# Start of a fused attention and MoE kernel: the first tile's queries loaded alone, the other head split on GpSimd, filler transposes

## The chip, the core and the metric

The kernel runs on one core of one Trainium2 chip. The metric is the device time of one execution in microseconds (us). Five engines work side by side, each through its own queue in order: TensorE (PE, with its weight loads as PEld), VectorE (DVE), ScalarE (ACT), GpSimd (POOL) and SyncE (SP), which here only issues DMAs.

## What is computed

Attention with pooled queries, then two MoE-like layers. Shapes: batch 2, 8 heads, 1152 keys, head size 64, 576 pooled queries per head.

```python
def _attn_ref(q, k, v):
    B, H, S, D = q.shape                       # 2, 8, 1152, 64
    q_pool = q.reshape(B, H, S // 2, 2, D).mean(axis=3)
    scores = (1 / np.sqrt(D)) * np.matmul(q_pool, k.transpose(0, 1, 3, 2))
    scores = scores - np.max(scores, axis=-1, keepdims=True)
    attn = np.exp(scores)
    attn = attn / (np.sum(attn, axis=-1, keepdims=True) + 1e-09)
    return np.matmul(attn, v)

x = attn_out.transpose(0, 2, 1, 3).reshape(B * S2, H * D)
h = x @ w_in;  x = np.maximum(0.01 * h, h) @ w_out        # 512 -> 2048 -> 512
p = probs / probs.sum(-1)
out = sum(p[:, e] * (np.maximum(x @ w1[e], 0) @ w2[e]) for e in range(4))
```

All operands are float32. The kernel splits each into a high part (rounded to the fp32r type) and a low part (the rest) and multiplies the parts.

## The kernel before

The attention works on 8 pairs of heads (batch x 4 pairs), each pair in 9 tiles of 128 query rows by 1152 keys: tiles 0 to 3 belong to head 0, tile 4 to both heads, tiles 5 to 8 to head 1. A running number i counts tiles over all pairs, so tile 9 is the first of pair 1. Per tile, with the names used below:

- **S(i)**, line 346: 6 matmuls (12 for tile 4 of pair 0) of queries and keys into three PSUM banks, which all tiles share; then the **eviction** on DVE (line 349), which scales into `e` and takes the row's extreme.
- **exp(i)** on ACT (line 355), a small sum on DVE (line 359), a reciprocal on DVE (line 363) and **norm(i)** on POOL (line 365).
- **T(i)**, line 386: 9 transposes on PE; ACT copies them out as the high part (line 390), DVE subtracts for the low part (line 98 through `lo`).
- The product with v (line 413), spread over later tiles; `done` (lines 421 to 424) writes `xh` and `xl`, on POOL for nearly all tiles.

The order on each engine is the order in which the program emits its instructions (`manual_schedule`). The main loop emits for step i: S(i+2) and its eviction (i+3 from i = 6 on, line 511), sum(i+1), T(i) with norm(i+1) behind its first three transposes, some products with v, exp(i+2), and then what `steps[i]` holds. `steps` are the pieces of preparing a later pair: `prep_pair(n)` gives a list of pieces, and `begin_at` says at which step the list starts (pair 0's v at step 0, pair 1 at step `P1` = 1, pair 2 at step 8). For pairs 1 and up the preparation is: pool the queries (`q_add`, POOL), high part of the keys (`k_hi`, ACT), low part (`k_lo`, POOL, one instruction of 128x1152, followed by four DMAs on SP that spread both parts over the partitions), `q_hi` (ACT), `q_lo` (DVE for pair 1, followed by four DMAs on SP), then v (`v_hi` ACT, `v_lo`). S(9) needs pair 1's key DMAs and the two DMAs of its queries of head 0; all stand in SP's one queue, keys first.

Pair 0 has a start of its own, `first_pair`: its queries and keys are loaded twice, to partitions 0 to 63 and to 64 to 127, by eight DMAs of 288 KB on SP in the order queries of head 0, keys of head 0, queries of head 1, keys of head 1, with v behind them. Then q_add, q_lo and k_lo of both heads run on DVE and q_hi and k_hi on ACT, all before the main loop, and v_lo of pair 0 runs on DVE. While the data comes, PE runs 28 filler transposes of the identity (line 449).

Of the kernel before, what the change touches and what calls it, by code (L numbers as in the profile page):

```python
# [11 lines left out]
F32 = mybir.dt.float32  # L12
# [15 lines left out]
CW = 384  # L28
# [5 lines left out]
def f32(ap):  # L34
    return ap.bitcast(F32)
# [3 lines left out]
def tile_kernel(ctx: ExitStack, tc: tile.TileContext, q, k, v, w_in, w_out, probs, w1, w2, out):  # L39
    nc = tc.nc  # L40
    PE, ACT, DVE, POOL, SP = nc.tensor, nc.scalar, nc.vector, nc.gpsimd, nc.sync

    def at(name, off, shape, dt=F32R):

        return nc.alloc_sbuf_tensor_at(name, [128, *shape], dt, offset=BASE + 4 * off).ap()
# [9 lines left out]
    qst = [at(f"qst{i}", 18432 + 2560 * i, [2, 2, SQ + 64]) for i in range(2)]  # L55
# [33 lines left out]
    def hi(eng, dst, src):  # L89
        if eng is ACT:  # L90
            ACT.copy(dst, src)  # L91
        elif eng is POOL:
            POOL.tensor_scalar(dst, src, 1.0, 1.0, op0=ALU.mult, op1=ALU.mult)
        else:
            DVE.tensor_copy(dst, src)

    def lo(eng, dst, src, high):
        eng.tensor_tensor(dst, src, f32(high), op=ALU.subtract)  # L98
# [53 lines left out]
    def load_a():  # L152
        f = next(a_next, None)
        if f is not None:
            SP.dma_start(wa_raw[f % 2], w_in[f].bitcast(I32))
# [37 lines left out]
    with ExitStack() as actx:  # L193
# [3 lines left out]
        def transposed():  # L197
            return PS[:, next(bank_t), :CW].rearrange("p (a b) -> p a b", a=3)
# [12 lines left out]
        def two_heads(n, name):  # L211
            return [kv[name, h, n % 2] for h in range(2)]

        def load_qk(n):
            if n >= len(pairs):
                load_a()
                load_a()
                return
            b, p = pairs[n]
            rk, rq = rk_b, rq_b.rearrange("p (a b) -> p a b", a=2)  # L220
            SP.dma_start(rk, k[b, p])
            SP.dma_start(rq, q[b, p])
            raw[n] = (rk, rq)

        def load_v(n):
            if n >= len(pairs):
                return
            b, p = pairs[n]
            raw_v[n] = rv_b.rearrange("p (a h d) -> p a h d", a=NKB, h=2)
            SP.dma_start(raw_v[n], v[b, p])  # L230

        def first_pair():

            b, p = pairs[0]
            ks = kst[0] = two_heads(0, "k")
            rk = [rk_b, e_b[4]]
            rq = [t.rearrange("p (a b) -> p a b", a=2) for t in (rq_b, e_b[3])]
            up, down = slice(0, 64), slice(64, 128)
            for h in range(2):
                src = slice(h * 64, h * 64 + 64)  # L240
                for d in (up, down):
                    SP.dma_start(rq[h][d], q[b, p, src])
                for d in (up, down):
                    SP.dma_start(rk[h][d], k[b, p, src])
            load_v(0)

            def q_add(h):
                DVE.tensor_tensor(rq[h][:, 0], rq[h][:, 0], rq[h][:, 1], op=ALU.add)

            def q_hi(h):  # L250
                hi(ACT, qst[0][:, 0, h, h * 64:h * 64 + SQ], rq[h][:, 0])

            def q_lo(h):
                cs = slice(h * 64, h * 64 + SQ)
                lo(DVE, qst[0][:, 1, h, cs], rq[h][:, 0], qst[0][:, 0, h, cs])

            def k_hi(h, c):
                cs = slice(c * CW, (c + 1) * CW)
                hi(ACT, ks[h][:, cs], rk[h][:, cs])

            def k_lo(h, c):
                cs = slice(c * CW, (c + 1) * CW)
                lo(DVE, ks[h][down, cs], rk[h][down, cs], ks[h][down, cs])
            return q_add, q_hi, q_lo, k_hi, k_lo

        def prep_pair(n):


            e_q, e_v = DVE if n == 1 else POOL, DVE if n == 0 else POOL
            rk, rq = raw.get(n, (None, None))  # L270

            def k_hi():
                kh = k_hi_of[n] = kh_b[n % 2]
                hi(ACT, kh, rk)

            def k_lo():
                kh = k_hi_of[n]
                ks = kst[n] = two_heads(n, "k")
                lo(POOL, rk.bitcast(F32R), rk, kh)
                for h in range(2):  # L280
                    r = slice(h * 64, h * 64 + 64)
                    SP.dma_start(f32(ks[h][0:64]), f32(kh[r]))
                    SP.dma_start(f32(ks[h][64:128]), rk[r])

            def q_add():
                POOL.tensor_tensor(rq[:, 0], rq[:, 0], rq[:, 1], op=ALU.add)

            def q_hi():
                hi(ACT, rq[:, 1].bitcast(F32R), rq[:, 0])

            def q_lo():
                lo(e_q, rq[:, 0].bitcast(F32R), rq[:, 0], rq[:, 1])
                t = qst[n % 2]
                for h in range(2):
                    r = slice(h * 64, h * 64 + 64)
                    hi(POOL, qmid[n % 2][r, r], rq[r, 0, (SQ - 64) * (1 - h):][:, :64])
                    for d in (slice(0, 64), slice(64, 128)):
                        SP.dma_start(f32(t[d, :, h, h * 64:h * 64 + SQ]), rq[r])

            def v_hi(h):  # L300
                if h == 0:
                    vst[n] = [t.rearrange("p (a b) -> p a b", a=NKB) for t in two_heads(n, "v")]
                a = h * 64
                hi(ACT, vst[n][h][:, :, a:a + 64], raw_v[n][:, :, h, :])

            def v_lo(h):
                a, c = h * 64, 64 - h * 64
                lo(e_v, vst[n][h][:, :, c:c + 64], raw_v[n][:, :, h, :], vst[n][h][:, :, a:a + 64])

            if n == 0:  # L310
                return [[lambda: v_hi(0)], [lambda: v_lo(0)], [lambda: v_hi(1)], [lambda: v_lo(1), lambda: load_v(1)]]
            return [[q_add, k_hi], [k_lo], [q_hi], [q_lo, lambda: load_qk(n + 1)], [lambda: v_hi(0)],
                    [lambda: v_lo(0), lambda: v_hi(1)], [lambda: v_lo(1), lambda: load_v(n + 1)]]

# [2 lines left out]

        AVD, AVB = 1.07, {1: 0.5}

        P0, P1, P2 = 10, 1, 8  # L320

        L2 = 6

# [115 lines left out]
                av.pop(0)[1]()  # L439

        with tc.manual_schedule():

            DVE.memset(warm, 0.0)
            ACT.activation(warm, warm, AF.Exp)
            q_add, q_hi, q_lo, k_hi, k_lo = first_pair()

            wps = transposed()
            for _ in range(28):
                PE.transpose(wps[:, 0], ident, ident)
            q_add(0)  # L450
            q_hi(0)
            q_lo(0)
            for c in range(3):
                k_hi(0, c)
                k_lo(0, c)
            q_add(1)
            q_hi(1)
            at = dict.fromkeys(("s", "exp", "sum", "norm"), 0)

            def upto(what, emit, i):  # L460
                first = {"exp": "s", "sum": "exp", "norm": "sum"}
                while at[what] <= i and at[what] < (at[first[what]] if what in first else len(tiles)):
                    emit(at[what])
                    at[what] += 1

            upto("s", emit_s, 0)
            upto("exp", emit_exp, 0)
            q_lo(1)
            for c in range(3):
                k_hi(1, c)  # L470
            upto("s", emit_s, 1)
            upto("sum", emit_sum, 0)
            upto("norm", emit_norm, 0)
            for c in range(3):
                k_lo(1, c)
            upto("exp", emit_exp, 1)
            load_qk(1)

# [24 lines left out]


            begin_at = {9 * m - P0: m for m in range(3, len(pairs))} | {0: 0, P1: 1, P2: 2}
            steps = {}
            for i, (n, t) in enumerate(tiles):
                if i in begin_at:
                    for d, fs in enumerate(prep_pair(begin_at[i])):
# [274 lines left out]
    with tc.manual_schedule():  # L784
# [24 lines left out]
        for what, *args in order:  # L809
            what(*args)  # L810
            if what is product:
                p, name = args
# [4 lines left out]
                elif name == "P2" and p or name == "P7" and p == NPAIR - 1:  # L817


                    n = p - (name == "P2")  # L820
# [31 lines left out]
```

## Time and profile before

| what | us |
|---|---|
| median of 3 runs | 868.78 (866.94 to 868.99) |
| the profiled execution | 866.99 |
| its span, first to last instruction | 865.2 |
| PE busy | 829.0 (96%) |
| DVE / ACT / POOL busy | 587.4 / 435.6 / 403.6 |

The span is cut into slices by some views, with the busy share of each engine, the clock granted to TensorE (1.00 is 2.4 GHz, 0.50 is 1.2 GHz) and what the DMAs moved. A timeline row gives start, duration, engine, line, operation, output <- input and count, and in brackets how long the engine had been idle and what released it. Rows of several instructions are merged: their duration is the sum or the stretch they cover.

### The profile page before, as it was taken

How to read it: one execution, taken by the hardware profiler on the slowest of the kernel's cores; microseconds unless marked ns; L12 is line 12 of the kernel's file. 1: busy time of each engine (PE TensorE's matmuls, PEld its weight loads, DVE VectorE, ACT ScalarE, POOL GpSimd, SP SyncE). 2: the span in 40 equal slices, each digit the busy share in tenths (PEclk: the TensorE clock that was granted, in tenths of full speed). 3: DMA queues.
4: the chain of work that ended last, by engine and by line, in shares of the span. 5: the costliest groups of instructions: out<-in, count | busy, mean ns of one | idle time of the engine just before them, and what ended most of it. 6: DMA issues, size and time to landing. Idle time of an engine off the chain costs nothing.

```text
span 865.2 us, 13539 instructions
## 1 busy us (share of the span) xinstructions
PE 829.0 (96%) x5071; PEld 777.9 (90%) x5071; DVE 587.4 (68%) x964; ACT 435.6 (50%) x762; POOL 403.6 (47%) x362
## 2 busy tenths in 40 slices
PE   6899999999989799999999899999999999999998
PEld 5789999999989799999999888889898898889886
DVE  5989999999998989877866662625444352625342
ACT  4889999999875565443333541505142241506030
POOL 1678988898744678556551330505032331404020
PEclk7999999999999999999999999999999999999999
DMA  6446545654501223322120210202011110201012
GB/s 192 111 123 179 136 113 151 178 125 123 153 26 50 98 98 98 98 98 74 57 91 1 72 51 1 98 1 73 26 49 49 49 50 1 98 0 49 1 37 98
DMA packets 25153, 68.65 MB, mean 79 GB/s; under 512 B 2944, under 2 KB 7040, under 8 KB 25088
## 3 DMA queue, kind: packets, MB, share of 16 engines
q1 hardware_dynamic: 25088, 67.79, 26.3%
q8 instruction: 40, 0.66, 0.3%
q14 instruction: 25, 0.20, 0.1%
HBM read 48.91 MB, written 2.36 MB: 59 GB/s over the span
## 4 chain that ended last, share of the span: by engine, by line
PE 75%; DVE 15%; ACT 4%; issue 3%; DMA 1%; POOL 1%; SPq 0%; DVEq 0%; ACTq 0%; POOLq 0%
PE ps L688 16%; PE ps L728 8%; PE ps L729 8%; PE ps L730 8%; PE ps L346 7%; PE ps L413 6%; PE ps L386 5%; DVE e L349 4%; PE ps L585 3%; PE ps L586 3%; PE ps L587 3%; PE ps L187 3%; PE ps L188 3%; PE ps L189 3%; DVE tl L98 2%
## 5 line engine op out<-in xcount | busy, mean ns | idle before, releaser
L98 POOL TENSOR_TENSOR bb<-w2r,bb 128x512 fp32r<-128x512 f32 x32 | 44.9, 1424 | 284.1 <-ACT bb L91 284.1
L688 PE MATMUL ps<-yT,ws 128*128 128x288 f32 x768 | 114.4, 300 | 10.6 <-ACT cb L707 10.6
L688 PEld LDWEIGHTS ps<-yT,ws 128*128 128x128 f32 x768 | 106.4, 191 | 15.1 <-ACT cb L707 14.9
L735 DVE SCALAR_TENSOR_TENSOR oacc<-ps,pw,oacc 128x512 f32<-128x512 f32 x63 | 47.2, 750 | 102.6 <-PE ps L730 102.6
L365 POOL TENSOR_SCALAR e<-e,st 128x1152 f32<-128x1152 f32 x70 | 86.8, 1243 | 57.4 <-DVE st L363 49.8
L98 DVE TENSOR_TENSOR tl<-ps,th 128x384 fp32r<-128x384 f32 (+1 forms) x240 | 112.0, 503 | 1.7 <-ACT th L390 1.7
L728 PE MATMUL ps<-bb,gg 128*128 128x512 f32 x288 | 112.2, 390 | 0.0
L729 PE MATMUL ps<-bb,gg 128*128 128x512 f32 x288 | 112.2, 389 | 0.0
L730 PE MATMUL ps<-bb,gg 128*128 128x512 f32 x288 | 112.1, 389 | 0.0
L346 PE MATMUL ps<-k,qst 128*128 128x384 f32 x438 | 97.2, 354 | 11.9 <-DVE e L349 6.7
L349 DVE TENSOR_SCALAR_CACHE_REDUCE e<-ps 128x1152 f32<-128x1152 f32 x72 | 97.4, 1353 | 16.3 <-PE ps L346 14.5
L390 ACT CAST th<-ps 128x384 fp32r<-128x384 f32 (+1 forms) x240 | 91.1, 458 | 23.8 <-PE ps L386 22.2
L355 ACT ACTIVATE e<-e,st 128x1152 f32<-128x1152 f32 x72 | 91.1, 1265 | 4.4 <-DVE e L349 2.7
L346 PEld LDWEIGHTS ps<-k,qst 128*128 128x128 f32 x438 | 77.4, 195 | 17.2 <-DVE e L349 11.9
L694 ACT COPY ca<-ps 128x576 f32<-128x576 f32 x16 | 10.3, 641 | 163.4 <-PE ps L688 155.0
L386 PE MATMUL ps<-ident,e 128*128 128x128 f32 x648 | 84.4, 275 | 3.8 <-POOL e L365 2.0
L688 PE MATMUL ps<-yB,ws 128*128 128x288 f32 x576 | 84.4, 296 | 0.0
L386 PEld LDWEIGHTS ps<-ident,e 128*128 128x128 f32 x648 | 75.0, 141 | 9.7 <-POOL e L365 5.0
L688 PEld LDWEIGHTS ps<-yB,ws 128*128 128x128 f32 x576 | 79.8, 189 | 0.5
L98 DVE TENSOR_TENSOR ws<-wf,ws 128x768 fp32r<-128x768 f32 (+1 forms) x32 | 41.5, 1297 | 55.5 <-ACT ws L91 55.5
L187 PE MATMUL ps<-xh,a 128*128 128x384 f32 x192 | 65.1, 339 | 4.1 <-DVE gf L564 4.1
L585 PE MATMUL ps<-g,b 128*128 128x384 f32 x192 | 64.4, 335 | 0.7 <-DVE gf L564 0.3
(126 smaller groups left out, 1728.2 us busy)
## 6 DMA issues: line engine op xcount, KB each, us to landing
wa<-in_w_in SPq DMA_DIRECT2D x16, 512.0 KB, 3.5
wb<-in_w_out SPq DMA_DIRECT2D x16, 512.0 KB, 4.3
wf<-in_w SPq DMA_DIRECT2D x32, 256.0 KB, 3.5
w2r<-in_w SPq DMA_DIRECT2D x16, 512.0 KB, 3.5
qst<-rq SPq DMA_DIRECT2D x28, 288.0 KB, 4.5
rv<-in_v SPq DMA_DIRECT2D x8, 576.0 KB, 5.3
rk<-in_k SPq DMA_DIRECT2D x7, 576.0 KB, 6.1
rq<-in_q SPq DMA_DIRECT2D x7, 576.0 KB, 4.7
```

The costliest lines, as they stand in the source:

```text
L98: eng.tensor_tensor(dst, src, f32(high), op=ALU.subtract)
L187: PE.matmul(ps[:, c, :CW], wh[:, k_], src_h[:, k_, cs], start=k_ == 0, stop=False)
L346: PE.matmul(ps[:, c, :CW], x, y, start=m == 0, stop=m == len(mms) - 1)
L349: DVE.tensor_scalar(e, ps[:, :, :CW], -0.5 / float(D) ** 0.5, None, op0=ALU.mult, op1=ALU.min, accum_out=st[:, 0:1])
L355: ACT.activation(e, e, AF.Exp, bias=st[:, 0:1], scale=-1.0, accum_out=st[:, 1:2])
L386: PE.transpose(ps[:, j], e[:, (3 * g + j) * 128:(3 * g + j + 1) * 128], ident)
L390: ACT.copy(h, ps[:, :, s0:s0 + w])
L585: PE.matmul(ps[:, c, :CW], wh, gh[:, cs], start=f == fs[0], stop=False)
L688: PE.matmul(ps[:, c, :HW], w[wi][:, i, ks], y[:, yi, k, c * HW:(c + 1) * HW], start=bool(first and k == 0 and m == 0), stop=k == 1 and m = ...
L728: PE.matmul(ps, gh[:, ts_], wh, start=f == fs[0], stop=False)
L729: PE.matmul(ps, gh[:, ts_], wl, start=False, stop=False)
L730: PE.matmul(ps, gl[:, ts_], wh, start=False, stop=f == fs[-1])
```

## The change

1. `first_pair` issues the 128 query columns of tile 0 alone (two DMAs of 64 KB), then head 0's keys. The DMAs to partitions 0 to 63 go out on SP, those to 64 to 127 on ACT. Behind them SP issues the rest of head 0's queries, then head 1's queries and keys, then v. The two ACT issues stand ahead of ACT's first activation. Head 1's raw data moves to other buffers (`rk1`, `rq1`).
2. The queries of head 0 are split in two parts: columns 0 to 127 by DVE and ACT before the keys, columns 128 to 575 later: q_add on POOL, q_hi on ACT, q_lo on DVE behind the eviction of S(0).
3. Head 1's q_add, q_lo and k_lo go from DVE to POOL, k_lo as one instruction of 64x1152, and with q_hi and k_hi (ACT) they move from ahead of the main loop into step 0, behind T(0), norm(1) and exp(2).
4. v_lo of pair 0 goes from DVE to POOL; v's pieces come at steps 1 and 2 instead of 0 to 3. Pair 1's preparation begins at step 2 instead of 1, with its first four pieces packed into three: q_lo and its DMAs stay at step 4, q_add and k_hi go from step 1 to 2, k_lo from 2 to 3; loading pair 1's v goes from step 3 to 2.
5. The 28 filler transposes become 20, with 14 more behind S(0) and 8 behind S(1).

```diff
+    rk1, rq1 = (at(f"r{i}1", 31872 + 2 * 2880 + 1152 * i, [S], F32) for i in range(2))
...
-            for h in range(2):
-                src = slice(h * 64, h * 64 + 64)
-                for d in (up, down):
-                    SP.dma_start(rq[h][d], q[b, p, src])
-                for d in (up, down):
-                    SP.dma_start(rk[h][d], k[b, p, src])
+            h0, h1 = up, down
+
+            SP.dma_start(rq[0][up, :, :128], q[b, p, h0, :, :128])
+            ACT.dma_start(rq[0][down, :, :128], q[b, p, h0, :, :128])
+            SP.dma_start(rk[0][up], k[b, p, h0])
+            ACT.dma_start(rk[0][down], k[b, p, h0])
+            for d in (up, down):
+                SP.dma_start(rq[0][d, :, 128:], q[b, p, h0, :, 128:])
+            for d in (up, down):
+                SP.dma_start(rq[1][d], q[b, p, h1])
+            for d in (up, down):
+                SP.dma_start(rk[1][d], k[b, p, h1])
             load_v(0)
...
-            e_q, e_v = DVE if n == 1 else POOL, DVE if n == 0 else POOL
+            e_q, e_v = DVE if n == 1 else POOL, POOL
...
             if n == 0:
-                return [[lambda: v_hi(0)], [lambda: v_lo(0)], [lambda: v_hi(1)], [lambda: v_lo(1), lambda: load_v(1)]]
+                return [[], [lambda: v_hi(0), lambda: v_lo(0)], [lambda: v_hi(1), lambda: v_lo(1), lambda: load_v(1)]]
+            if n == 1:
+                return [[q_add, k_hi], [k_lo, q_hi], [q_lo, lambda: load_qk(n + 1)], [lambda: v_hi(0)],
+                        [lambda: v_lo(0), lambda: v_hi(1)], [lambda: v_lo(1), lambda: load_v(n + 1)]]
             return [[q_add, k_hi], [k_lo], [q_hi], [q_lo, lambda: load_qk(n + 1)], [lambda: v_hi(0)],
...
-        P0, P1, P2 = 10, 1, 8
+        P0, P1, P2 = 10, 2, 8
...
-            q_add, q_hi, q_lo, k_hi, k_lo = first_pair()
-
             wps = transposed()
-            for _ in range(28):
-                PE.transpose(wps[:, 0], ident, ident)
-            q_add(0)
-            q_hi(0)
-            q_lo(0)
+
+            def keep_warm(n):
+
+                for _ in range(n):
+                    PE.transpose(wps[:, 0], ident, ident)
+            keep_warm(20)
+            q_add(DVE, 0, 0, 128)
+            q_hi(0, 0, 128)
+            q_lo(DVE, 0, 0, 128)
             for c in range(3):
-                k_hi(0, c)
-                k_lo(0, c)
-            q_add(1)
-            q_hi(1)
+                k_hi(0, c * CW, (c + 1) * CW)
+                k_lo(DVE, 0, c * CW, (c + 1) * CW)
...
+            q_add(POOL, 0, 128, SQ)
             upto("s", emit_s, 0)
+            q_hi(0, 128, SQ)
+            keep_warm(14)
             upto("exp", emit_exp, 0)
-            q_lo(1)
-            for c in range(3):
-                k_hi(1, c)
-            upto("s", emit_s, 1)
+            q_lo(DVE, 0, 128, SQ)
             upto("sum", emit_sum, 0)
             upto("norm", emit_norm, 0)
-            for c in range(3):
-                k_lo(1, c)
+            upto("s", emit_s, 1)
+            keep_warm(8)
             upto("exp", emit_exp, 1)
             load_qk(1)
...
-            steps = {}
+            steps = {0: [lambda: q_add(POOL, 1, 0, SQ), lambda: q_hi(1, 0, SQ), lambda: q_lo(POOL, 1, 0, SQ),
+                         lambda: k_hi(1, 0, S), lambda: k_lo(POOL, 1, 0, S)]}
```

## Rows read from the trace of the kernel before

**Rows 1.** Page, busy time of the engines and the granted clock in 40 slices

```profile
PE 829.0 (96%) x5071; PEld 777.9 (90%) x5071; DVE 587.4 (68%) x964; ACT 435.6 (50%) x762; POOL 403.6 (47%) x362
PEclk7999999999999999999999999999999999999999
```

**Rows 2.** Stretches: from:to, length, busy us (instructions) per engine, clock, DMA share, GB/s

```profile
4.50:5.00 0.50, 0.50 (x4) 0.50 (x4) 0.00 (x0) 0.00 (x0) 0.00 (x0) 1.00 0.98 230
9.50:10.00 0.50, 0.50 (x2) 0.47 (x3) 0.50 (x2) 0.08 (x1) 0.00 (x0) 0.50 0.77 175
14.50:15.00 0.50, 0.50 (x3) 0.37 (x2) 0.00 (x0) 0.50 (x2) 0.00 (x0) 0.50 1.07 433
23.00:23.25 0.25, 0.25 (x2) 0.15 (x2) 0.00 (x0) 0.25 (x3) 0.04 (x1) 0.71 0.00 0
43.00:44.00 1.00, 0.00 (x0) 0.00 (x0) 0.52 (x2) 0.00 (x0) 0.00 (x0) 1.00 0.92 270
50.00:60.00 10.00, 9.85 (x71) 9.45 (x69) 8.68 (x26) 9.36 (x19) 8.94 (x9) 1.00 0.26 66
```

**Rows 3.** Timeline from 0 to 25 us

```profile
1.46 5.50 PE L449 MATMUL ps<-ident 128*128 128x128 f32 x28 [1.46 <-POOL ident masks.py:199]
8.24 1.34 ACT L91 CAST k<-rk 128x384 fp32r<-128x384 f32 x3 [1.05 <-DMA rk<-in_k]
9.40 2.23 PE L346 MATMUL ps<-k,qst 128*128 128x384 f32 x6 [2.43 <-DVE k L98]
11.67 1.36 DVE L349 TENSOR_SCALAR_CACHE_REDUCE e<-ps 128x1152 f32<-128x1152 f32 x1
16.84 2.29 PE L346 MATMUL ps<-k,qst 128*128 128x384 f32 x6 [1.46 <-DVE e L349]
19.17 2.18 PE L386 MATMUL ps<-ident,e 128*128 128x128 f32 x9
21.81 1.23 POOL L365 TENSOR_SCALAR e<-e,st 128x1152 f32<-128x1152 f32 x1 [2.70 <-DVE st L363]
24.73 2.38 PE L346 MATMUL ps<-k,qst 128*128 128x384 f32 x12 [0.43 <-DVE e L349]
```

**Rows 4.** The fillers of line 449 in two stretches: min/median/max ns, first and last start

```profile
L449 PE MATMUL ps<-ident x2: 421/421/421, 5.6 to 5.8; 128*128 128x128 f32 x2
L449 PE MATMUL ps<-ident x3: 272/272/273, 6.4 to 6.6; 128*128 128x128 f32 x3
```

**Rows 5.** Timeline from 25 to 49 us: steps at full clock, and GpSimd

```profile
29.25 1.21 PE L346 MATMUL ps<-k,qst 128*128 128x384 f32 x6
26.65 1.93 POOL L286 TENSOR_TENSOR rq<-rq 128x576 f32<-128x576 f32 x1
29.33 1.25 POOL L365 TENSOR_SCALAR e<-e,st 128x1152 f32<-128x1152 f32 x1 [0.75 <-ACT th L390]
30.52 2.69 POOL L98 TENSOR_TENSOR rk<-rk,kh 128x1152 fp32r<-128x1152 f32 x1
34.37 0.92 POOL L93 TENSOR_SCALAR xh<-xf 64x256 fp32r<-64x256 f32 x1
35.37 0.72 POOL L98 TENSOR_TENSOR xl<-xf,xh 64x256 fp32r<-64x256 f32 x1
33.72 1.30 DVE L98 TENSOR_TENSOR v<-rv,v 128x576 fp32r<-128x576 f32 x1
48.94 1.42 POOL L98 TENSOR_TENSOR v<-rv,v 128x576 fp32r<-128x576 f32 x1
```

**Rows 6.** Timeline, SyncE's issues of pair 1's DMAs, and S(9)

```profile
33.24 0.48 SPq L283 DMA_DIRECT2D k<-rk  x1
34.42 0.76 SPq L283 DMA_DIRECT2D k<-rk  x1
39.75 0.60 SPq L298 DMA_DIRECT2D qst<-rq  x1
44.15 1.31 PE L346 MATMUL ps<-k,qst 128*128 128x384 f32 x6 [2.13 <-DVE e L349]
```

More of the change, by code (lines that the diff above doesn't have):

```diff
@@ L235, in first_pair @@
             ks = kst[0] = two_heads(0, "k")
-            rk = [rk_b, e_b[4]]
-            rq = [t.rearrange("p (a b) -> p a b", a=2) for t in (rq_b, e_b[3])]
+            rk = [rk_b, rk1]
+            rq = [t.rearrange("p (a b) -> p a b", a=2) for t in (rq_b, rq1)]
             up, down = slice(0, 64), slice(64, 128)
-            for h in range(2):
-                src = slice(h * 64, h * 64 + 64)
-                for d in (up, down):
-                    SP.dma_start(rq[h][d], q[b, p, src])
-                for d in (up, down):
-                    SP.dma_start(rk[h][d], k[b, p, src])
@@ L245, in first_pair @@
-            load_v(0)
[L247 to L259, printed above, removed]
@@ L261, in k_lo @@
-            def k_lo(h, c):
-                cs = slice(c * CW, (c + 1) * CW)
-                lo(DVE, ks[h][down, cs], rk[h][down, cs], ks[h][down, cs])
+            h0, h1 = up, down
[5 more added lines that the diff above has]
+                SP.dma_start(rq[0][d, :, 128:], q[b, p, h0, :, 128:])
@@ new lines, in first_pair, with q_add, q_hi, q_lo @@
+            for d in (up, down):
+                SP.dma_start(rq[1][d], q[b, p, h1])
+            for d in (up, down):
+                SP.dma_start(rk[1][d], k[b, p, h1])
+            load_v(0)
+            def q_add(e, h, a, z):
+                e.tensor_tensor(rq[h][:, 0, a:z], rq[h][:, 0, a:z], rq[h][:, 1, a:z], op=ALU.add)
+            def q_hi(h, a, z):
+                hi(ACT, qst[0][:, 0, h, h * 64 + a:h * 64 + z], rq[h][:, 0, a:z])
+            def q_lo(e, h, a, z):
+                cs = slice(h * 64 + a, h * 64 + z)
+                lo(e, qst[0][:, 1, h, cs], rq[h][:, 0, a:z], qst[0][:, 0, h, cs])
@@ L264, in first_pair, with k_hi, k_lo @@
+            def k_hi(h, a, z):
+                hi(ACT, ks[h][:, a:z], rk[h][:, a:z])
+            def k_lo(e, h, a, z):
+                lo(e, ks[h][down, a:z], rk[h][down, a:z], ks[h][down, a:z])
             return q_add, q_hi, q_lo, k_hi, k_lo
         def prep_pair(n):
-            e_q, e_v = DVE if n == 1 else POOL, DVE if n == 0 else POOL
+            e_q, e_v = DVE if n == 1 else POOL, POOL
             rk, rq = raw.get(n, (None, None))
@@ L441, in tile_kernel @@
         with tc.manual_schedule():
+            q_add, q_hi, q_lo, k_hi, k_lo = first_pair()
             DVE.memset(warm, 0.0)
             ACT.activation(warm, warm, AF.Exp)
-            q_add, q_hi, q_lo, k_hi, k_lo = first_pair()
             wps = transposed()
-            for _ in range(28):
-                PE.transpose(wps[:, 0], ident, ident)
-            q_add(0)
-            q_hi(0)
-            q_lo(0)
+            def keep_warm(n):
[5 more added lines that the diff above has]
+            q_lo(DVE, 0, 0, 128)
             for c in range(3):
-                k_hi(0, c)
-                k_lo(0, c)
-            q_add(1)
-            q_hi(1)
+                k_hi(0, c * CW, (c + 1) * CW)
+                k_lo(DVE, 0, c * CW, (c + 1) * CW)
             at = dict.fromkeys(("s", "exp", "sum", "norm"), 0)
```

## The prediction

> **What bounds the kernel now.** The page comes first: TensorE is busy 96% of the span, and its clock is below full only in the first slice of 21.6 us [rows 1]. From 50 us on a stretch of 10 us holds 9.85 us of matmuls [rows 2]; there the order on TensorE is the bound, and what comes before simply shifts it. So the change, which touches the first 45 us only, is worth the shift of S(9), the first tile of pair 1, which starts at 44.15 [rows 6]. Next, the timeline of the start. The keys' cast begins at 8.24 after a wait for their DMA, S(0) runs at 9.40, its eviction at 11.67 [rows 3]. The fillers end at 6.96; 2.4 us later S(0) starts, and at once the granted clock goes from 1.00 to 0.50, which it keeps until 23.1 [rows 2, 3]. (The profile shows 1.00 from the first instant, but the fillers take 421 ns until about 5.8 us and 272 ns after it [rows 4], so TensorE really was at half clock until near 6 us.) It rose at 23.1 when TensorE had worked without a gap since 19.17 [rows 2, 3]. At half clock S takes 2.29 us, at full clock 1.21 [rows 3, 5]. Last, the waits ahead of S(9): TensorE does nothing from 43 to 44 us while the DMAs run [rows 2]. S(9) starts 4.4 us after the second issue of pair 1's queries at 39.75 [rows 6], and that is what it waits for; the eviction named beside it had ended at 43.5.
>
> **Keys earlier.** The bytes ahead of the last of head 0's keys fall from 1.18 MB to 0.72 MB (288 KB four times, against 64 KB twice and 288 KB twice). DMAs to 64 partitions move 230 GB/s, those of 128 partitions 433 [rows 2]. Taken at about 240, the nearest row in form, 0.46 MB less is 1.9 us: the cast starts at 6.3 instead of 8.24. If the two queues fill both halves of the partitions at once and reach 433, 0.72 MB take 1.7 us behind the first byte at about 2.0, and with the 1.4 us that the landing of the keys lags behind their bytes before, the cast starts at 5.1. No load here runs on two queues, so 5.1 to 6.5 are the bounds and 6.3 is taken. The Trainium skill speaks against more ("SBUF — State Buffer", section "Can I just issue two DMAs to hit both halves?"): two DMAs, one to each half, together gave only 6% over one. By it the cast would start at 6.2. ACT's two issues, some 0.6 us each by SP's [rows 6], delay its table load, which ends long before the queries need ACT: the first tile's q_add, q_hi and q_lo (about 0.3 us each for 128 columns) fit ahead of the keys. Cost nothing, and 0.5 us if the keys came at 5.1.
>
> **S(0) to norm(1).** From the cast to the eviction of S(0) took 3.43 us [rows 3], the last two matmuls at half clock. At full clock I take off 0.75: eviction at 9.0. Then eviction (1.4) and q_lo of the other 448 columns (0.6) stand ahead of S(1): 11.1. The 14 fillers take 1.5 us at the 0.11 us apart of full clock and are hidden beside these; at half clock (0.21) they take 3.0 and cost 0.9. S(1), its eviction, S(2) and its eviction follow each other through the one set of PSUM banks, each 1.4 us: S(2) at 13.9, its eviction at 15.3, and norm(1) 2.1 us behind the start of that, as in before (19.55 to 21.81 with 0.1 of waiting): norm(1) from 17.4 to 18.65, where it was 21.81 to 23.04 [rows 3]. So far 4.4 us are won, 2 by the keys and the rest by the clock.
>
> **Head 1 behind norm(1).** This is where I see it lost. GpSimd gets q_add, q_lo and k_lo of head 1 in a row behind norm(1). Prices: a two-input GpSimd instruction takes 1.42 us for 576 columns and 2.69 for 1152 [rows 5]; I take 1.45 each for q_add and q_lo (1.93 was seen beside a DVE instruction with two inputs, of which there are few now), 2.69 for k_lo, as 64 partitions should not be shorter than 128 (xl, on 64, has the same cost per column [rows 5]), and 0.9 for q_hi on ACT between them with two hand-overs. Sum 6.5: S(4), which needs all of it, starts at 25.15. In before it started at 24.73 [rows 3], since head 1 was ready long before. Behind the waiting q_hi on ACT stand T(1)'s copies, exp(3) and through them sum and reciprocal; that costs nothing, because norm(2) stands behind k_lo on GpSimd anyway. On TensorE T(2) and the product with v stand behind S(4): it is done with T(1) at 19.85 and idles 5.3 us. In before, 2.4 us of idling were followed by half clock [rows 2, 3], so I expect half clock at S(4): its 12 matmuls take 4.6 (twice 2.29) instead of 2.4, ending at 29.75 instead of 27.1. If the clock holds, 27.55.
>
> **Pair 1 through GpSimd.** From the end of S(4) the queue on GpSimd is: 2.2 us to norm(3) (27.1 to 29.33 in before), norm(3) 1.25, v_lo of head 1 1.42 (with some 0.45 of waiting for v_hi, which comes behind exp(4)), q_add 1.45, norm(4) 1.25, xh and xl 1.64, k_lo 2.69 [rows 5]. Sum 12.3: k_lo ends at 42.05; in before it ended at 33.2 [rows 5]. DVE loses two v_lo, one measured at 1.30 us [rows 5], which were on the way in before and are worth about 1 us at S(6), but GpSimd is now the later one: norm(5) stands behind k_lo too. The DMAs: SP issued three of pair 1's four key DMAs behind k_lo (33.24 to 35.2) and the queries only at 39.06 [rows 6], with q_lo on DVE in between, so the keys had 5 us to land. Now q_lo is done long before, and five DMAs of 288 KB (three of keys, two of queries) stand in one row behind k_lo: 1.1 us to the first byte, 1.47 MB at 250 GB/s 5.9 us, some 0.9 to land: 7.9. (The least is 2.5 of issues and the 4.4 seen before S(9), 6.9.) S(9) starts at 49.95 instead of 44.15: **5.8 us later**. What is late next, T(6) and all behind it, stands behind S(9) on TensorE, as before.
>
> **The sum.** On the profiled execution's 866.99 us (its span of 865.2 and 1.8 around it) this gives 872.8. The median of the runs is 868.78, near the upper of the three, and the forecast is for a median: 868.78 + 5.8 = **874.6**.
>
> **Rivals.**
> *The clock falls twice, or is low at the start (longer).* Ahead of S(9) TensorE would idle some 3 us again; resuming at half clock for 4 us, as from 19.17 to 23.1 [rows 3], loses 2: 876.6. And 20 fillers at 0.21 us end at 5.75, just short of the moment at which the clock rose under 28 [rows 4]; if it does not rise, S(0) and the fillers behind it run at half clock and norm(1) ends 1.2 later. Both: 877.8. For it: 2.4 us of idling were enough once; against it: 2.1 us ahead of S(9) were not [rows 6]. Chance 0.28.
> *Both halves at once and a clock that holds (no change that can be told).* Keys at 5.1 (1.2 less) and S(4) at full clock (2.2 less): 874.6 - 3.4 = 871.2. For it, the 433 GB/s of full-width loads; against it, 5.3 us of idling. Chance 0.11.
> *Head 1 fits into GpSimd's idle time (not slower).* The place is GpSimd's queue between norm(0), ending at about 13.5, and norm(1) at 17.4: if the pieces ran there, they would end near 20, S(4) would start at about 21.2 at full clock and end at 23.6, and S(9) would follow 12.3 + 7.9 later at 43.8: 868.4. It decides whether the first q_add of head 1 runs before or after norm(1); the program's order says after. Chance 0.08.
> *The start-up gain reaches the end (faster).* As the last, and pair 1's DMAs land while TensorE still works through T(5) and S(8), so that TensorE's own order sets S(9), some 16.9 us behind the end of S(4): 40.5, 3.7 earlier, 865.1. For that GpSimd's pieces between norm(3) and k_lo would have to cost half of their rows. Chance 0.08.
>
> **How the numbers follow.** About 0.3% (2.6 us) is what a measurement of this kernel can tell from no change. The forecast with its single fall of the clock has 0.45, the longer rival 0.28: slower 0.73. The rivals at 871.2 and 868.4 make 0.19 for no change, the last 0.08 for faster. The range runs from 870.5, which takes in the first of the shorter rivals, to 879.0, the longest sum and a little for GpSimd's 1.93 us in place of 1.45; it leaves out about 0.16.
>
> **What would show it.** In the profile after: the keys' cast at 5.1 to 6.5; norm(1) near 17.4; q_add, q_lo and k_lo of head 1 on GpSimd behind it, and TensorE idle for some 5 us until S(4) at about 25; half clock there; k_lo of pair 1 ending near 42; five DMAs behind it and S(9) near 50. From S(9) to the end the two traces should be alike; if S(9) moves by another amount than the total, the last step is wrong. The forecast falls if GpSimd's pieces overlap (S(4) before 23), or if k_lo of pair 1 is done by 36, since then TensorE's order sets S(9).

## The result, and the profile after

The changed kernel takes **873.92 us** (median of 6 runs, 871.46 to 875.39) against 867.72 before (6 runs, 866.06 to 868.99): a ratio of 1.0068, 95% interval 1.0048 to 1.0089. It is slower by 6.2 us. The profiled execution took 874.08, of which the span is 872.3; before it was 865.2 [rows 1]. The rows below answer to those of before. First the page, busy time per engine and the granted clock in 40 slices:

```profile
span 872.3 us, 13567 instructions
PE 830.4 (95%) x5085; PEld 779.8 (89%) x5085; DVE 583.5 (67%) x958; ACT 435.6 (50%) x761; POOL 411.6 (47%) x368
PEclk9989999999999999999999999999999999999999
```

The first digit rose from 7 to 9, but the third fell to 8: there is now a stretch of low clock between 43.6 and 65.4 us as well. The timeline of the start, which answers to [rows 3] (line 355 is S, 358 its eviction, 374 norm, 256 q_add and 100 the low parts):

```profile
7.15 1.34 ACT L93 CAST k<-rk 128x384 fp32r<-128x384 f32 x3 [3.08 <-DMA rk<-in_k]
9.93 3.11 PE L460 MATMUL ps<-ident 128*128 128x128 f32 x14
10.17 1.36 DVE L358 TENSOR_SCALAR_CACHE_REDUCE e<-ps 128x1152 f32<-128x1152 f32 x1 [0.97 <-PE ps L355]
19.04 1.24 POOL L374 TENSOR_SCALAR e<-e,st 128x1152 f32<-128x1152 f32 x1 [4.30 <-DVE st L372]
20.23 1.42 POOL L256 TENSOR_TENSOR r<-r 128x576 f32<-128x576 f32 x1
21.29 0.60 PE L355 MATMUL ps<-k,qst 128*128 128x384 f32 x2
22.43 1.40 POOL L100 TENSOR_TENSOR qst<-r,qst 128x576 fp32r<-128x576 f32 x1 [0.78 <-ACT qst L93]
23.91 2.62 POOL L100 TENSOR_TENSOR k<-r,k 64x1152 fp32r<-64x1152 f32 x1
26.59 3.51 PE L355 MATMUL ps<-k,qst 128*128 128x384 f32 x10 [4.70 <-POOL k L100]
```

The keys' cast is 1.1 us earlier than before and norm(1) 2.8 us earlier. Then three instructions of GpSimd stand in a row. S(4) is torn in two by them: the first two of its 12 matmuls, which belong to head 0, run at 21.29; the other ten wait for head 1, TensorE idles 4.7 us, and they start at 26.59, 1.9 us later than S(4) started before. Where S(4) is torn in this way, its start below is that of the ten. The stretches show what the idling does to the clock (from:to, length, busy us and count per engine, clock, DMA share, GB/s; the third number from the end is the clock):

```profile
9.50:10.00 0.50, 0.50 (x3) 0.40 (x3) 0.00 (x0) 0.00 (x0) 0.50 (x1) 0.50 1.09 230
22.00:24.00 2.00, 0.00 (x0) 0.00 (x0) 0.18 (x1) 2.00 (x4) 1.49 (x2) 1.00 0.00 0
27.00:28.00 1.00, 1.00 (x4) 1.00 (x4) 0.00 (x0) 0.00 (x0) 1.00 (x2) 0.50 0.00 0
30.00:31.00 1.00, 1.00 (x11) 1.00 (x10) 0.86 (x1) 0.53 (x2) 0.00 (x0) 1.00 0.00 0
44.00:45.00 1.00, 1.00 (x6) 1.00 (x5) 1.00 (x5) 1.00 (x3) 0.00 (x0) 0.50 1.00 281
49.00:50.00 1.00, 0.01 (x1) 0.04 (x1) 0.21 (x2) 0.00 (x0) 0.00 (x0) 1.00 1.07 251
50.50:52.00 1.50, 1.50 (x7) 1.40 (x6) 0.00 (x0) 0.00 (x0) 0.00 (x0) 0.50 1.02 244
54.00:55.00 1.00, 1.00 (x9) 1.00 (x8) 0.94 (x3) 1.00 (x2) 0.79 (x1) 1.00 0.85 313
```

After 20 us TensorE stands still three times (from 21.9, from 39.9 and from 47.8, see the bracketed waits in the timelines), and each time the clock falls to 0.50 at the moment it works again or within 1 us of it, until about 30, 46.5 and 53.8. The middle fall did not hold S(9): the eviction of S(8) ended at 49.2, and S(9)'s queries landed at 49.7. The timeline around pair 1's keys and S(9), which answers to [rows 5, 6]:

```profile
38.77 2.65 POOL L100 TENSOR_TENSOR rk<-rk,kh 128x1152 fp32r<-128x1152 f32 x1
40.49 2.73 DVE L100 TENSOR_TENSOR rq<-rq 128x576 fp32r<-128x576 f32 x1
41.40 1.22 POOL L374 TENSOR_SCALAR e<-e,st 128x1152 f32<-128x1152 f32 x1
41.45 0.48 SPq L289 DMA_DIRECT2D k<-rk  x1
42.62 0.76 SPq L289 DMA_DIRECT2D k<-rk  x1
42.68 1.39 PE L395 MATMUL ps<-ident,e 128*128 128x128 f32 x9 [2.73 <-POOL e L374]
43.49 4.89 SPq L304 DMA_DIRECT2D qst<-rq  x4
49.99 1.93 PE L355 MATMUL ps<-k,qst 128*128 128x384 f32 x6 [2.18 <-DMA qst<-rq]
```

S(9) starts at 49.99, **5.84 us later** than before. From S(9) to the end it is 822.3 (872.3 - 49.99) against 821.05: **1.26 more**. Together 7.1 us of span. The profile's chain of waits passes through these pieces, among others (start, us, what):

```profile
19.04 1.24 POOL e L374
20.28 1.38 POOL r L256
23.91 2.63 POOL k L100
26.59 3.52 PE ps L355 x10
44.77 4.97 DMA qst<-rq
49.99 1.93 PE ps L355 x6
```

### The profile page after: what moved, and what is told of

Read it like the earlier page. It is cut to its first block, busy times and chain, and to the rows that moved or that the text cites. A ratio compares the mean times of both kernels' runs of the same rounds, so it can differ in the third digit from the quotient of the medians.

```text
span 872.3 us, 13567 instructions
## 1 busy us (share of the span) xinstructions
PE 830.4 (95%) x5085; PEld 779.8 (89%) x5085; DVE 583.5 (67%) x958; ACT 435.6 (50%) x761; POOL 411.6 (47%) x368
## 3 DMA queue, kind: packets, MB, share of 16 engines
HBM read 48.91 MB, written 2.36 MB: 59 GB/s over the span
## 4 chain that ended last, share of the span: by engine, by line
PE 73%; DVE 16%; ACT 4%; issue 3%; POOL 2%; DMA 2%; SPq 0%; DVEq 0%; ACTq 0%; POOLq 0%
PE ps L699 16%; PE ps L740 8%; PE ps L739 7%; PE ps L741 7%; PE ps L355 7%; PE ps L422 6%; PE ps L395 5%; PE ps L597 3%; PE ps L596 3%; PE ps L598 3%; DVE e L358 3%; PE ps L189 2%; PE ps L190 2%; PE ps L191 2%; DVE tl L100 2%
## 5 line engine op out<-in xcount | busy, mean ns | idle before, releaser
L374 POOL TENSOR_SCALAR e<-e,st 128x1152 f32<-128x1152 f32 x70 | 86.3, 1237 | 48.8 <-DVE st L372 43.6
```

The source lines that it names most:

```text
L374: eng.tensor_scalar(e, e, st[:, 3:4], 1.0, op0=ALU.mult, op1=ALU.mult)
```

## The experiments

The theory: head 1's split on GpSimd holds S(4); GpSimd's queue behind S(4) holds pair 1's k_lo; a row of DMAs behind it holds S(9). The rivals: S(4)'s delay is absorbed later; GpSimd's queue is not what sets S(9); the rest of the loss is the clock. "S(9)" is its start, "tail" the time from there to the end of the profiled span. The kernel before had S(9) at 44.15 and a tail of 821.05. The medians are of 2 to 12 runs; each kernel has one profiled execution, and its S(4), k_lo, S(9) and tail are of that one.

| kernel | median us | ratio to before [95%] | S(4) | k_lo of pair 1 ends | S(9) | tail |
|---|---|---|---|---|---|---|
| changed | 873.92 | 1.0068 [1.0048, 1.0089] | 26.59 | 41.42 | 49.99 | 822.3 |
| e1_head1_dve | 868.91 | 1.0018 [1.0003, 1.0032] | 22.18 | 36.26 | 44.87 | 823.1 |
| e3_p1 | 871.00 | 1.0046 [1.0031, 1.0061] | 27.81 | 38.92 | 49.29 | 820.8 |
| e5_late | 874.18 | 1.0076 [1.0059, 1.0092] | 27.04 | 43.12 | 51.70 | 820.9 |
| e5_gap | 874.64 | 1.0082 [1.0065, 1.0100] | 25.66 | 41.37 | 49.95 | 823.9 |
| e4_order | 871.40 | 1.0067 [1.0041, 1.0093] | 26.14 | 41.82 | 48.85 | 820.6 |
| e6_fill | 874.84 | 1.0099 [1.0079, 1.0119] | 25.38 | 38.69 | 48.73 | 823.1 |
| e7_onequeue | 873.47 | 1.0082 [1.0054, 1.0110] | 26.49 | 42.18 | 50.77 | 820.7 |
| e8_best | 868.03 | 1.0021 [1.0006, 1.0037] | 21.88 | 31.96 | 45.62 | 820.2 |
| e10_start | 865.48 | 0.9982 [0.9967, 0.9997] | 21.80 | 30.50 | 41.50 | 820.7 |
| e9_early | 864.18 | 0.9968 [0.9954, 0.9981] | 23.24 | 32.97 | 43.13 | 819.4 |

**e1_head1_dve: head 1's split back on DVE, in its gaps ahead of the main loop.**

```diff
             q_lo(DVE, 0, 128, SQ)
+            q_add(DVE, 1, 0, SQ)
+            q_hi(1, 0, SQ)
...
+            q_lo(DVE, 1, 0, SQ)
             upto("s", emit_s, 1)
             keep_warm(8)
+            k_hi(1, 0, S)
             upto("exp", emit_exp, 1)
+            k_lo(DVE, 1, 0, S)
...
-            steps = {0: [lambda: q_add(POOL, 1, 0, SQ), lambda: q_hi(1, 0, SQ), lambda: q_lo(POOL, 1, 0, SQ),
-                         lambda: k_hi(1, 0, S), lambda: k_lo(POOL, 1, 0, S)]}
+            steps = {}
```

> The changed kernel, with head 1's q_add, q_lo and k_lo back on DVE, put into DVE's gaps ahead of step 0 (behind the evictions of S(0) and S(1)); all else as changed. Theory (GpSimd's row behind norm(1) holds S(4) back, and the idling in front of it costs the clock): S(4) at about 21.5 instead of 26.6, at full clock, ending at 24 instead of 30.1; pair 1's k_lo and S(9) follow 6 us earlier, S(9) near 44; total 6 us less, near 868. Rival (the time is lost behind S(4) alone, in GpSimd's work for v and pair 1, which has room to wait): S(9) moves by less than 2 us.

Timeline of this kernel:

```profile
19.94 1.23 POOL L374 TENSOR_SCALAR e<-e,st 128x1152 f32<-128x1152 f32 x1 [5.55 <-DVE st L372]
22.18 2.36 PE L355 MATMUL ps<-k,qst 128*128 128x384 f32 x12
33.62 2.64 POOL L100 TENSOR_TENSOR rk<-rk,kh 128x1152 fp32r<-128x1152 f32 x1
44.87 2.26 PE L355 MATMUL ps<-k,qst 128*128 128x384 f32 x6 [3.75 <-DMA qst<-rq]
```

S(4) runs in one piece, without a wait and at full clock (2.36 us for 12 matmuls); it starts 4.4 us earlier than the ten did and ends 5.6 earlier, and S(9) follows 5.1 earlier; the median is 5.0 lower. So this one part of the change costs 5 us, and nearly nothing absorbs it on the way to S(9). The price on the other side is smaller: norm(1) is 0.9 later, although S(0) had started 0.4 earlier in this execution. What is left of the loss against before is 0.7 at S(9) and 2.0 in the tail, where S(9) runs at half clock (2.26) after 3.75 us of idling.

**e3_p1: pair 1's preparation a step earlier and in four pieces, as in before.**

```diff
-                return [[q_add, k_hi], [k_lo, q_hi], [q_lo, lambda: load_qk(n + 1)], [lambda: v_hi(0)],
+                return [[q_add, k_hi], [k_lo], [q_hi], [q_lo, lambda: load_qk(n + 1)], [lambda: v_hi(0)],
...
-        P0, P1, P2 = 10, 2, 8
+        P0, P1, P2 = 10, 1, 8
```

> The changed kernel, with pair 1's preparation beginning at step 1 again, in its four separate pieces; head 1 and v stay on GpSimd. Theory (k_lo of pair 1 and its DMAs set S(9), through GpSimd's order): q_add falls into GpSimd's wait ahead of norm(3), k_lo runs ahead of norm(4) and ends near 37.7 instead of 41.4, its DMAs are out before the queries', S(9) starts 2 to 3 us earlier, near 47.5; S(4) stays at 26.6; total 2 to 3 us less. Rival (S(9) is set by TensorE's order or by DVE's q_lo): S(9) moves less than 0.5 us.

Counted from S(4), which came 1.2 late in this execution, k_lo of pair 1 ends 3.7 us earlier (11.11 behind S(4) instead of 14.83) but S(9) only 1.9 earlier (21.48 instead of 23.40). The bound has passed on: q_lo runs on DVE at 42.99 to 44.05, long after the keys went out, and the queries are issued at 44.12. The key DMAs had their head start, as in before [rows 6], and now the queries are late alone.

**e5_late and e5_gap: the same extra GpSimd addition of 128x576, ahead of pair 1's k_lo, or at step 1 behind v_lo.**

```diff
+            def extra():
+                r = raw[1][0]
+                POOL.tensor_tensor(xl[:, 3, 576:1152], r[:, :576], r[:, :576], op=ALU.add)
...
-                return [[q_add, k_hi], [k_lo, q_hi], [q_lo, lambda: load_qk(n + 1)], [lambda: v_hi(0)],
+                return [[q_add, k_hi], [extra, k_lo, q_hi], [q_lo, lambda: load_qk(n + 1)], [lambda: v_hi(0)],
```

(In e5_gap it stands in pair 0's list instead, behind `v_lo(0)`.)

> The changed kernel, with one more GpSimd addition of 128x576 (1.42 us, into a place that is written later) right ahead of pair 1's k_lo. Theory (GpSimd's queue is full from norm(3) to k_lo and sets S(9)): k_lo ends and S(9) starts 1.4 us later, total plus 1.4, more if the clock falls otherwise. Rival (GpSimd has room there): nothing moves.

> The changed kernel, with the same extra GpSimd addition of 1.42 us placed behind v_lo of head 0 at step 1, where GpSimd waits 2.96 us for norm(3). Theory (only work in the full part of GpSimd's queue costs time): S(9) and the total stay, within 0.3 us. Rival (any GpSimd work costs its length, by contention or otherwise): plus 1.4.

The addition took 1.14 us in one and 1.15 in the other. Ahead of k_lo it moved S(9), counted from S(4), by 1.26; at step 1 it lay in idle time, as the timeline of e5_gap shows (its line 280 is the addition, 378 norm), where norm(3) still waits 1.92 us behind it:

```profile
28.27 1.15 POOL L280 TENSOR_TENSOR xl<-rk 128x576 fp32r<-128x576 f32 x1
31.34 1.24 POOL L378 TENSOR_SCALAR e<-e,st 128x1152 f32<-128x1152 f32 x1 [1.92 <-DVE st L376]
```

So up to norm(3) the extra instruction cost nothing: norm(3) starts 5.68 us behind S(4), in the changed kernel 5.61. S(9), counted from S(4), still came 0.89 later in e5_gap, but 0.84 of that is a longer wait of v_lo for ACT's v_hi (0.99 instead of 0.15 us), and e4_order and e7_onequeue, which have no addition, show the same 0.99. In all three T(4) ran wholly at half clock (2.12 us, in the changed kernel 1.14). GpSimd's queue is the bound from norm(3) to k_lo of pair 1, and not from S(4) to norm(3).

The totals don't follow S(9): both are within 0.8 us of the changed kernel. In e5_late the clock held at S(9) and the tail is 820.9; in e5_gap S(9) took 2.26 us at half clock after 3.75 of idling and the tail is 823.9. The tail differs by 3 us, more than the step that was tested, and 2.5 of it lie between S(9) and S(10), the next tile (3.30 and 5.83 us).

**e4_order: SP issues the keys and queries of head 0 first, the keys of head 1 behind them.**

```diff
-                for h in range(2):
+                for h in range(1 if n == 1 else 2):
+                    k_out(h)
...
                         SP.dma_start(f32(t[d, :, h, h * 64:h * 64 + SQ]), rq[r])
+                    if n == 1 and h == 0:
+                        k_out(1)
```

> The changed kernel, with SP's order of pair 1 changed: head 0's two key DMAs, then head 0's two query DMAs, and head 1's keys and queries behind them, so that S(9) needs three DMAs of 288 KB behind k_lo instead of five. If the DMA row alone sets S(9), it starts 2.4 us earlier (0.59 MB at 250 GB/s). If TensorE's order sets it too (norm(5) stands behind k_lo on GpSimd, T(5) behind norm(5), S(8) behind T(5), and S(8)'s eviction ended at 49.2, 0.8 ahead of S(9) at 50.0), it moves by 0.8 at the most; total 0 to 0.8 less.

From the end of k_lo to S(9) it took 7.03 instead of 8.57, so the bytes ahead of the queries cost 1.5 us, neither the full gain nor none. The queries did not go out earlier: they are issued at 43.71, when DVE's q_lo has ended (timeline of e4_order, in which S is line 361 and norm 380):

```profile
40.93 2.70 DVE L100 TENSOR_TENSOR rq<-rq 128x576 fp32r<-128x576 f32 x1
41.80 1.22 POOL L380 TENSOR_SCALAR e<-e,st 128x1152 f32<-128x1152 f32 x1
43.71 1.28 SPq L308 DMA_DIRECT2D qst<-rq  x2
48.85 2.23 PE L361 MATMUL ps<-k,qst 128*128 128x384 f32 x6 [2.19 <-DMA qst<-rq]
```

In the changed kernel SP gets to the queries at 43.49, held almost equally by its key issues (until 43.38) and by q_lo (until 43.22). Taking one of them away leaves the other.

**e6_fill: fillers in TensorE's idle stretches (40 at step 2, 20 at step 5, 14 at step 6).**

```diff
+                if i == 6:
+                    upto("s", emit_s, 8)
+                for _ in range({2: 40, 6: 14}.get(i, 0)):
+                    PE.transpose(PS[:, 6 if i == 6 else 7, :128], ident, ident)
                 upto("s", emit_s, i + lead)
+                for _ in range(20 if i == 5 else 0):
+                    PE.transpose(PS[:, 6, :128], ident, ident)
```

> The changed kernel, with filler transposes in TensorE's three long idle stretches (40 ahead of S(4), 20 ahead of T(5), 14 between S(8) and S(9)). Theory (the clock falls because TensorE idles, and half clock costs S(4) 1.1 us and what follows S(9) 1.3 us): S(4) takes 2.4 us instead of 3.5, S(9) 1.3 instead of 1.9, total 2 to 3 us less, near 871.5. Rival (the clock costs nothing that the waits would not cost anyway): total within 0.5 us of the changed kernel's.

This missed. The first half came true: the ten matmuls of S(4) run at full clock in 2.02 us instead of 3.51, so half clock had cost 1.5 there and not the 1.1 of the expectation. k_lo of pair 1 ends at 38.69, 2.7 earlier: 1.2 of that is an earlier S(4), which the start of this execution gave, and 1.5 the clock. But S(9) is only 1.3 earlier, which is no gain counted from S(4) (23.35 us instead of 23.40), and the median is no lower. The DMAs gave the 1.5 back; this is the view of `qst` in the changed kernel, and then in e6_fill:

```profile
L304 SPq DMA_DIRECT2D qst<-rq x4: 1050/1218/1277, 43.5 to 47.2; - x4
DMA to landing us min/median/max: 4.9/5.0/5.0
```

```profile
L304 SPq DMA_DIRECT2D qst<-rq x4: 610/1264/1694, 40.8 to 45.1; - x4
DMA to landing us min/median/max: 5.3/6.4/6.5
```

From the issue of S(9)'s second query DMA to its landing the engines moved 238 GB/s in e6_fill and 243 in the changed kernel, so they were not slower, and more of other data went ahead; why stays open. And behind the last fillers TensorE still idled 3.67 us before S(9), which ran at half clock (2.26 us).

**e7_onequeue: the two DMAs that the change put on ACT go out on SP.**

```diff
-            ACT.dma_start(rq[0][down, :, :128], q[b, p, h0, :, :128])
+            SP.dma_start(rq[0][down, :, :128], q[b, p, h0, :, :128])
             SP.dma_start(rk[0][up], k[b, p, h0])
-            ACT.dma_start(rk[0][down], k[b, p, h0])
+            SP.dma_start(rk[0][down], k[b, p, h0])
```

> The changed kernel, with the two DMAs of ACT's queue back on SP's, in the same order of data. If two queues add no rate (two DMAs, one to each half, share what one has), the keys' cast starts within 0.4 us of the 7.15 us of the changed kernel. If they fill both halves at once, it starts 1 us later or more. Total within 1 us either way.

The keys' cast starts at 7.28 against 7.15 with two queues, and the medians are 0.5 apart. Executions differ by more: in the ten profiled kernels with two queues the cast stands between 6.36 (e5_gap) and 7.65 (e3_p1). The second queue is worth nothing that can be told from one profiled execution of each.

**e8_best and e10_start: only the start of the change.** e8_best has e1's edit and e3's, and v_lo of pair 0 on DVE again, still at steps 1 and 2; e10_start differs from it by one line:

```diff
-                return [[], [lambda: v_hi(0), lambda: v_lo(0)], [lambda: v_hi(1), lambda: v_lo(1), lambda: load_v(1)]]
+                return [[lambda: v_hi(0)], [lambda: v_lo(0)], [lambda: v_hi(1)], [lambda: v_lo(1), lambda: load_v(1)]]
```

> Only the start of the change: first tile's queries ahead, two queues, the split in two parts and the fillers; head 1's q_add, q_lo and k_lo on DVE in its gaps ahead of step 0, v_lo of pair 0 on DVE and pair 1's preparation at step 1 in four pieces, as in the kernel before. Theory (the start wins 2 to 3 us, and GpSimd's added work loses more): S(4) at 22 instead of 24.7 in the kernel before, S(9) near 41.6 instead of 44.15, total 2 to 2.5 us under the kernel before, near 865. Rival (what the start wins is taken back by another wait ahead of S(9), a DMA or DVE): within 1 us of the kernel before.

> As e8_best, but v of pair 0 prepared at steps 0 to 3 as in the kernel before, so that v_lo of head 1 on DVE stands at step 3, no longer beside GpSimd's k_lo. Theory (a DVE instruction with two SBUF inputs does not run while GpSimd's instruction runs: v_lo took 3.25 us in e8_best and ended 0.6 behind k_lo): v_lo takes 1.3 us, S(6) starts 2 us earlier than in e8_best (33.9), S(9) 1.5 to 2.5 us earlier than its 45.6; total 1.5 to 2.5 us under e8_best's 868.0, some 1 to 2 us under the kernel before. Rival (the 3.25 us were a wait for v_hi or data): v_lo as long as before, no gain.

e8_best missed its forecast: S(9) at 45.62. Its timeline shows where:

```profile
29.31 2.65 POOL L100 TENSOR_TENSOR rk<-rk,kh 128x1152 fp32r<-128x1152 f32 x1
29.32 3.25 DVE L100 TENSOR_TENSOR v<-rv,v 128x576 fp32r<-128x576 f32 x1 [0.46 <-ACT v L93]
32.49 1.34 DVE L358 TENSOR_SCALAR_CACHE_REDUCE e<-ps 128x1152 f32<-128x1152 f32 x1
33.90 2.29 PE L355 MATMUL ps<-k,qst 128*128 128x384 f32 x6 [2.47 <-DVE e L358]
```

v_lo, 1.30 us in before [rows 5], takes 3.25 beside GpSimd's k_lo, the eviction stands behind it on DVE, TensorE idles 2.47 and S(6) runs at half clock. With v's pieces as in before (e10_start) v_lo takes 1.47, S(9) comes at 41.50, 4.1 earlier, where 1.5 to 2.5 were expected, and the median falls by 2.6 to 865.48. The start of the change alone, with head 1 split in DVE's gaps, gains 2.2 us on the 867.7 of before in the same runs; the interval of its ratio, 0.9967 to 0.9997, only just leaves out no gain.

**e9_early: a version that beats both.** Head 1 as in e1; pair 1 is prepared from step 0, its queries first, its k_lo at step 2, its v behind.

```diff
-                return [[], [lambda: v_hi(0), lambda: v_lo(0)], [lambda: v_hi(1), lambda: v_lo(1), lambda: load_v(1)]]
+                return [[], [lambda: v_hi(0), lambda: v_lo(0)], [lambda: v_hi(1)], [lambda: v_lo(1), lambda: load_v(1)]]
...
-                return [[q_add, k_hi], [k_lo, q_hi], [q_lo, lambda: load_qk(n + 1)], [lambda: v_hi(0)],
+                return [[q_add, k_hi], [q_hi], [q_lo, k_lo], [], [lambda: load_qk(n + 1)], [lambda: v_hi(0)],
...
```

> The changed kernel, with head 1 split on DVE ahead of step 0 (as e1_head1_dve) and pair 1 prepared as early as its data allows: q_add on GpSimd and k_hi at step 0, q_hi at step 1, q_lo (DVE) and k_lo (GpSimd) at step 2, v_lo of head 1 and loading v put back to step 3. Theory (S(9) is set by GpSimd's k_lo and the DMAs behind it): S(4) at 22.2 as in e1_head1_dve, k_lo ends near 30.6 instead of 36.3, the DMAs land before TensorE needs them, S(9) near 41 by TensorE's order, no stop of TensorE ahead of it; total 2.5 to 3.5 us under the kernel before, near 864. Rival (TensorE or DVE then sets S(9) no earlier than in the kernel before): S(9) at 44 or later, no gain.

864.18, or 0.9968 [0.9954, 0.9981] of before, faster by 3.5 us. S(9) came 2 us later than expected, 1.0 of it already at S(4) (23.24 for 22.2), ahead of which S(3) ran at half clock (2.22 us). But no DMA holds S(9) any more (timeline of e9_early):

```profile
29.63 3.70 SPq L304 DMA_DIRECT2D qst<-rq  x4
43.13 1.33 PE L355 MATMUL ps<-k,qst 128*128 128x384 f32 x6 [1.55 <-DVE e L358]
```

It waits for an eviction and runs at full clock, and the tail is the shortest of all, 819.4. Of the 2.7 us by which its span is shorter than before's (862.5 and 865.2) only 1.0 is S(9); the rest lies in the tail, and why stays open. Its interval and that of e10_start overlap, so the order between these two is not settled.

## Why the prediction was right

Forecast 874.6, measured 873.92; S(9) was forecast at 49.95 and came at 49.99. The path was right, but the closeness is luck. The terms were off by both signs and cancelled: the keys +0.85, S(0) to norm(1) +0.8, head 1 -0.2, S(4) -1.1, GpSimd's row -1.0, the DMAs +0.7. The total was counted from 868.78, which is 1.06 above the median of the six runs, and left out the clock's fall behind S(9).

**Keys earlier: mis-sized, mostly beyond its bounds.** Forecast 6.3 within 5.1 to 6.5, measured 7.15 here, and 6.36 to 7.65 over the ten kernels that start alike; only e5_gap lies within the bounds. Pricing by bytes left out something in how the transfers begin. In the changed kernel the DMAs moved only 92 GB/s from 3.0 to 3.5 us, between the small loads of queries and the keys:

```profile
3.00:3.50 0.50, 0.50 (x5) 0.50 (x4) 0.05 (x1) 0.49 (x2) 0.00 (x0) 1.00 0.71 92
```

In e5_gap the same half microsecond moved 267 GB/s, and there the keys came as forecast. But that is not the whole of it: e4_order moved 92 GB/s as well and had its keys at 6.75, e3_p1 moved 175 and had them at 7.65. The cause stays open. The rival in which two queues fill both halves at once (5.1) is out: no kernel came near it, and e7_onequeue does as well within that spread. The Trainium skill ("SBUF — State Buffer", section "Can I just issue two DMAs to hit both halves?") says that issuing from several engines doesn't help, and the trace agrees as far as that spread lets one see: 7.15 with two queues against 7.28 with one. Its 6% for a second DMA was not tried, since every kernel here issues two for the keys.

**S(0) to norm(1): 1.64 late (19.04 for 17.4).** 0.85 of it are the keys. The rest is the clock, which fell at about 9.4 and came back near 12.8: the 14 fillers took 3.11 us, the 3.0 that the prediction named for half clock, and delayed S(1) by 0.5 of the 0.9 it allowed. Other kernels with the same order bear the price out, from the keys' cast to norm(1): 11.09 us in e6_fill, where these 14 fillers ran at full clock (1.69 us), for a forecast of 11.1; 11.89 in the changed kernel; 12.62 in e3_p1 and 12.77 in e5_late, where S(0) took 2.29 and the fillers 3.19. So the other half of rival 1, a low clock at the start, was partly true: the first 20 fillers did end at half clock (421 ns each), but S(0)'s first four matmuls still ran at full clock here (338 to 443 ns, the last two 522 and more). In e3_p1 and e5_late it was wholly true.

**Head 1 behind norm(1): right.** From the end of norm(1) to S(4) took 6.3 us for 6.5 forecast, and 64 partitions were indeed no shorter than 128 (2.62 us for 1152 columns, against 2.65 for pair 1's k_lo). TensorE idled 4.7 and fell to half clock, as forecast. But "S(4), which needs all of it" was wrong for its first two matmuls, which had run at 21.29; the other ten took 3.5 us where the forecast had 4.6 for 12: the term was mis-sized by 1.1. It was not the clock's rise at 29.9, since in e4_order, e5_gap and e7_onequeue, where T(4) behind them still ran at half clock, the ten took 3.57. e1_head1_dve shows the whole part by itself.

**Pair 1 through GpSimd: right, with two terms off.** From the end of S(4) (30.1) to the end of k_lo took 11.3 for 12.3: xh took 0.41 instead of the 0.92 of [rows 5] (there DVE's v_lo ran beside it), and v_lo hardly waited. From k_lo to S(9) took 8.57 for 7.9: three key issues and the first query issue bring SP to 44.77, the second query's DMA lands 4.97 later, and 0.25 follow. The sentence "q_lo is done long before" was wrong: q_lo ran at 40.49 to 43.22, beside GpSimd, and held the queries almost as long as the keys did. It cost nothing extra here, but e3_p1 and e4_order show that it is the next bound at once.

**From S(9) on: rival 1 came true.** The forecast took the two traces to be alike there; TensorE idled 2.2 us and fell to half clock until 53.8. This is S(10), in before and in the changed kernel:

```profile
47.45 1.23 PE L346 MATMUL ps<-k,qst 128*128 128x384 f32 x6
```

```profile
54.88 1.23 PE L355 MATMUL ps<-k,qst 128*128 128x384 f32 x6
```

From S(9) to S(10) it took 4.89 us instead of 3.30, so the fall cost 1.6 where the rival said 2; behind S(10) the changed kernel was 0.3 shorter, and 1.26 is what is left in the tail. The other kernels bear this out: 3.3 us where the clock held at S(9) (e3, e5_late, e7, e8, e9, e10), 4.89 in e4, 5.6 to 5.8 in e1, e5_gap and e6. The tail alone would mislead: e4's is short (820.6) although its clock fell. From S(10) to the end it took 815.7 in e4 and 816.0 in e9, and 816.9 to 818.0 in all others; nothing here explains these two.

In before 2.1 us of idling at the same place did not lower the clock [rows 6], and in e5_late 1.85 us did not. After 3.7 (e1, e5_gap, e6) it fell each time. Between them it went both ways: it fell after about 2.2 us in the changed kernel and in e4_order, and held after 2.2 in e3_p1, e8_best and e10_start and after 2.46 in e7_onequeue. How long TensorE idled there hung on its clock before. In e1 and e5_gap it ran T(5) and S(8) at full clock, was done sooner, idled 3.75 us for the same row of DMAs and lost 2.3 to 2.5 at S(9). In the changed kernel, e5_late and e7 it ran the work from T(5) on partly at half clock, idled 1.85 to 2.46 and lost 1.6 or nothing.

**The parts of the change** follow from the medians, each against before in its own runs: the start alone -2.2 (e10_start), pair 1's later preparation with v_lo on GpSimd and v's pieces at other steps 3.6 (e1 at +1.4 against e10 at -2.2), head 1's split on GpSimd 4.8 (the changed kernel at +6.2 against e1 at +1.4). By the intervals in the table each is uncertain by one to two us, and they hold for this order of undoing. How the 3.6 divide among its edits was not tried.

## What to carry to other kernels

Work moved to an engine that has spare time on average costs most of its length if it lands in a row ahead of something that the bottleneck engine waits for (here a row of 6.3 us moved S(4) by 4.4 and the total by 5): look at that engine's queue in that stretch, not at its share of the span. A gain at the start reaches the end only if the next hand-over (here the DMAs behind one low part) moves with it, and where two things hold the same issue, undoing one shows only a part of the price. Where idling lowers TensorE's clock, a wait can cost more than its length (here 1.6 to 2.5 us more at S(9)); where another wait follows, as at T(5), the low clock can be hidden.

## What the runs showed of the hardware

**A DVE instruction with two inputs in SBUF that ran beside a GpSimd instruction ended 0.6 us behind it.** q_lo of 128x576 took 1.06 us in before, at 37.93 beside a norm that ended at 38.39, and so ended 0.60 behind it. In the changed kernel it took 2.73 and ended 0.60 behind norm(5) (43.22 and 42.62); in e1 2.74 and 0.61; in e4 2.70 and 0.61; in e8 v_lo took 3.25 and ended 0.61 behind k_lo. Evictions, which read PSUM, keep their 1.34 to 1.36 us. In the changed kernel, e1 and e4 q_lo began beside k_lo and was passed by norm(5) as well, which started behind k_lo; in e5_late q_lo (41.02 to 43.74) ended 0.62 behind k_lo, and norm(5) gave way, with 1.74 us instead of 1.23. The Trainium skill ("SBUF — State Buffer", section "Who interferes with whom") states that a DVE instruction with two SBUF inputs contends with a GpSimd instruction that reads SBUF, and the trace agrees. The prediction had used this for GpSimd's prices alone, not for DVE's.
